# LSH attention feeding a gated MLP on one core: first late weight set fetched in the last heads, late pools with waits by tile, two orders of loads changed

## The chip, the cores and the metric

The kernel runs on one core of a Trainium2 chip. The metric is the device time of one execution in microseconds, with the median over runs. The engines are named as the profile names them: PE (TensorE matmuls), PEld (its weight loads), DVE (VectorE), ACT (ScalarE), POOL (GpSimd) and SP (SyncE, which here issues nearly all DMAs).

## The reference

Attention over 4 batches of 8 heads, 768 positions and 64 columns, masked to pairs whose hash buckets agree, and behind it a gated MLP on the 3072 tokens.

```python
q_bits = (np.einsum('bhsd,dk->bhsk', q, proj) > 0)          # 6 bits, and the same for k
mask = q_bucket[:, :, :, None] == k_bucket[:, :, None, :]
scores = np.where(mask, scale * np.matmul(q, k.transpose(0, 1, 3, 2)), -1e9)
attn = np.exp(scores - np.max(scores, axis=-1, keepdims=True))
attn = attn / (np.sum(attn, axis=-1, keepdims=True) + 1e-09)
x = np.matmul(attn, v)                                       # to (3072, 512)
gate = 1.0 / (1.0 + np.exp(-(x @ w_gate)))                   # w_gate, w_val: 512 x 1536
out = (gate * (x @ w_val)) @ w_out                           # w_out: 1536 x 512
```

q, k, v and the projection are fp32; the three MLP weights are passed as 64-bit floats.

## The kernel before, in words

**Precision.** Each fp32 operand of a large product is split in a high and a low fp32r part, and a product takes three matmuls (low times high, high times low, high times high). This is why each tile below comes as a pair: `xh` and `xl`, `a11h` and `a11l`, `gh` and `gl`. The high part is a cast on ACT, the low part a subtraction on POOL or DVE.

**Attention (first half of the program).** Sixteen pairs of heads `(b, hp)` run one after the other, each in two groups `g` of three query tiles, so 96 score steps in all. A step is `sc` (PE), `e` (DVE, the maximum and a copy), the exponent (ACT); a group then is turned (`tp`, PE), copied (`ef`, ACT or DVE) and multiplied with v (`pv`, PE). The group's row sums go to DRAM and come back broadcast (`rd`, then `rb`, both DMAs from SP), POOL multiplies `xs` with `rb`, and a DMA stores the result as `xd`, the attention output turned. Names end in batch, head pair and group: `xs3_3_1` is the last.

**Weight preparation, in the gaps of attention.** Each of 12 column blocks per matrix is loaded (`raw`, 512 KB), converted from 64-bit integers to fp32 (`ex`, `mf`; DVE, ACT, POOL in turn), split in two and, for the blocks `J1` = 2 and up, stored to DRAM (`kg`, `kv`, `ko`). Blocks of gate and value are first combined in pairs, as the 7-product scheme below wants them. Ten of 12 blocks are prepared during attention, the last two in the late half. `W_KEY` = 12 is the score step at which the first of them becomes due, and `W_STEP` = 2.2 the distance.

**Early MLP units.** Eight units `(b, g)` of 384 tokens compute the share of the first two 128-wide column blocks: `load_x` fetches `xr` (two DMAs of 384 KB) from `xd` and splits it to `xh` and `xl`; then come `zg` and `zv` (PE, L500; two blocks each, 12 matmuls per block), the gate, `gh` and `gl`, and `zo` (PE, L533; three token tiles of 6 matmuls), stored as `part`. The first six fill gaps of attention. The last two, `3_0` and `3_1`, come after the last head: `3_1` needs `xr3_1`, whose buffer is free only when POOL has made the last `xl` of `3_0`.

**Late MLP (second half).** The other ten column blocks are taken in five sets of two, three sets in phase 0 and two in phase 1; in each phase the four batches follow one another (`moe_pair`). A batch's x is loaded as four blocks `ra11`, `ra12`, `ra21`, `ra22` (384 KB each), and four sums of them (`s1` to `s4`) are made, for the 7-product (Strassen-Winograd) scheme: per set and matrix seven steps `z1` to `z7` of 6 matmuls (L719), in the order 1, 2, 5, 6, 3, 7, 4. `yo` (L838) is the product with w_out. The first set of the first batch is block pair 4: `z1g` and `z2g` need only a11 and a12 of batch 0 and the piece `wg0_4`. `fetch_piece` loads a set's ten pieces (two times three of 512 KB and one of 256 KB, and two of 512 KB: 4608 KB).

**What sets the order.** The whole program is put in order before it is built, by `Plan`: tasks with keys, modelled durations, dependencies and a stock of buffers are laid on the five engines, and each engine then executes its list strictly in that order. A wait in front of one instruction holds all that stands behind it on the same engine; SP's list of DMAs is one of these.

**The switch between the halves.** Attention's pools (`attn`, `stage1`, PSUM `ps2`) are held by the stack `ph1`. The task `switch` closes them and opens the late pools `latex`, `latet`, `latew` and `ps3` in the same memory. It runs when all `xd` stores (`every`) and all prepared weights (`early_kept`) are done, and all late fetches come after it.

```python
later["switch"] = add(0, "sp", 0, switch, after=every + early_kept, give=["moe"] * 2)
```

Of the kernel before, what the change touches and what calls it, by code (L numbers as in the profile page):

```python
# [42 lines left out]
class Task:  # L43
# [7 lines left out]
    def __init__(self, key, options, after, take, give, tail, kind):  # L51
        self.key, self.options, self.take, self.give, self.tail = key, options, take, give, tail
        self.kind, self.tiles = kind, DIVISION[kind]
        self.started, self.then, self.waits = False, [], 0
        for a in after:
            if a is not None:
                a.then.append(self)
                self.waits += 1
        self.ready = 0


class Plan:
# [9 lines left out]
    def add(self, key, engine, ns=None, emit=None, after=(), take=(), give=(), tail=0, kind="all"):  # L72
        options = engine if isinstance(engine, list) else [(engine, ns, emit)]
        t = Task((key, len(self.tasks)), options, after, take, give, tail, kind)
        self.tasks.append(t)
        return t

    def order(self):
# [24 lines left out]
        while events:  # L103
# [10 lines left out]
            while again:  # L114
                again = False
                for e in SEEN:
# [39 lines left out]
                    for r in t.give:  # L156
                        at(seen, "give", r)
                    for a in t.then:
# [11 lines left out]
def lsh_attention_glu_kernel(ctx, tc, q, k, v, proj, w_gate, w_val, w_out, out):  # L170
# [84 lines left out]
    stage1 = ph1.enter_context(tc.tile_pool(name="stage1", bufs=1))  # L255
# [18 lines left out]
    stock = dict(  # L274
        one=1, two=3, moe=1, z=6, kr=2, qr=2, vr=2, h=2, e=12, st=3, su=3, sv=2, rb=2, xs=2,
        ef=4, qx=1, kx=1, raw1=1, cv1=1, wk1=2, raw2=1, cv2=1, wk2=1, xr=1, x=1, ob=3, ol=3, sn=4, sg=6, gf=4, sc=1, port=1,
# [27 lines left out]
    def converted(key, n, j, late, which, after, first):  # L304
# [9 lines left out]
        def load():  # L314
            z["raw"] = raw = stage().tile([P, 2 * N_EL], I32, name=f"raw{n}{j}", tag="wraw")
# [223 lines left out]
    def moe_early(key, b, g, stored, pace):  # L539
# [8 lines left out]
        for j in range(J1):  # L548
# [6 lines left out]
            ))  # L555
        if direct:
# [38 lines left out]
        return prev, last_z  # L595
# [3 lines left out]
    def x_pair(u, b, last_use):  # L599
# [38 lines left out]
        def raw(name):  # L638
            got[name] = dma(
                FIRST, 393216, lambda: load(name), after=stored[b, int(name[1]) - 1] + [later["switch"]], take=[f"r{name}"],  # L640
            )
# [22 lines left out]
        pieces_of("a12")  # L664
# [14 lines left out]
    def fetch_piece(at_, js, slot, n, m, after, first):  # L679

        def go():
# [3 lines left out]
            else:  # L685
                to = later["x"].tile([P, 2, size], F32R, name=f"w{n}{m}_{js[0]}_{at_[0]}{at_[1]}", tag=f"w{slot}{n}{m}")
# [7 lines left out]
            after=[made_piece[key_], later["switch"], last_fetch.get(role)] + after, take=[role],  # L694
# [208 lines left out]
    score_tasks = {}  # L903
# [10 lines left out]
    def pair(i):  # L914
# [6 lines left out]
        def load(n, eng):  # L921

            if n == "k":
                z[n] = at.tile([P, 2, GT, 2, D], F32, name=f"kr{u}", tag="kr", bufs=stock["kr"])
# [4 lines left out]
            else:  # L929
                z[n] = at.tile([P, NC, 2, D], F32, name=f"qr{u}", tag="qr", bufs=stock["qr"])  # L930
# [22 lines left out]
        def plain_(n, eng):  # L953
            z[n + "x"] = at.tile([P, S], F32, name=f"{n}x{u}", tag=f"{n}x", bufs=1)
# [72 lines left out]
        for m, n in enumerate("qk"):  # L1027
# [5 lines left out]
            add(0, "sp", 0, lambda: None, after=[c_, a], give=[n + "x"])  # L1033
            needs.append(c_)
# [171 lines left out]

    units = [(b, g) for b in range(B) for g in range(NG)]
    PARTS = 2 * J1 + GT
    for m, (b, g) in enumerate(units):
# [6 lines left out]
        last_early, last_x = moe_early(1e4 + m, b, g, stored[b, g], [p if p is None else score_tasks[p] for p in pace])  # L1216
# [16 lines left out]
    for i, sets in enumerate(PHASES):  # L1233
        for b in range(B):
            for js, slot in sets:
                alone = sum(x[1] == slot for x in sets) == 1
                for n, m in PIECES:
                    if alone and b:
                        made[(i, b), js, n, m] = made[(i, 0), js, n, m]
                    else:  # L1240
                        fetch_piece((i, b), js, slot, n, m, [last_early] if (i, b) == (0, 0) and slot == 1 else [], (i, b) == (0, 0))
# [34 lines left out]
```

## Time and profile before

| what | value |
|---|---|
| median of 3 runs (lowest to highest) | 1017.61 us (1016.65 to 1025.71) |
| the profiled execution's own time | 1016.87 us |
| its span, first to last instruction | 1014.9 us |
| PE, DVE, ACT, POOL busy | 979.6, 762.2, 559.9, 288.2 us |
| attention's last `pv` ends, late half's last store lands | about 513 us, about 1011 us |

A profile's page gives the busy time of each engine, then the span in 40 equal slices (25.4 us each) with a digit for tenths of busy time; `PEclk` is the TensorE clock granted in a slice. A row of the timeline has a start and a duration in us, engine, line, operation, the tiles out and in, and in brackets how long the engine had been idle before and what released it. A row of the windows view has, for one stretch, its length, the busy time of each engine with the number of instructions, the granted clock, the busy share of the DMA engines and the GB/s moved. Line numbers are those of the kernel before.

### The profile page before, as it was taken

What the parts mean: (1) busy time and instruction counts of PE and PEld (TensorE: products, weight loads), DVE (VectorE), ACT (ScalarE), POOL (GpSimd) and SP (SyncE); (2) the same over time, 40 slices, a digit from 0 to 9 for tenths busy, and PEclk for the clock granted to TensorE, in tenths of its full rate; (3) what the DMA queues carried; (4) which work ended last, traced back from release to release, by engine and by line L of the source; (5) the groups of instructions that cost most, each with busy time, mean ns of one, the idle gap of its engine ahead of it and who ended that gap; (6) DMA issues with size and microseconds to landing.
All of it is one profiled execution on the core that took longest, in us unless ns stands there. A gap on an engine that the chain in (4) does not pass through costs nothing.

```text
span 1014.9 us, 20971 instructions
## 1 busy us (share of the span) xinstructions
PE 979.6 (97%) x8108; PEld 779.9 (77%) x8108; DVE 762.2 (75%) x1412; ACT 559.9 (55%) x1022; POOL 288.2 (28%) x259
## 2 busy tenths in 40 slices
PE   7999999999999999999979999999999999999998
PEld 3665566676666666675668989999989989999897
DVE  2878997898777778887615787888787778787864
ACT  1778787877677778887644352343233325242430
POOL 4024346555554366463443121211000000000000
PEclk9999999999999999999998999999999999999999
DMA  7355666576775668645467977588359671505021
GB/s 159 90 148 147 168 170 176 183 227 180 219 200 190 183 179 261 184 144 184 167 245 261 383 285 258 203 281 310 140 185 385 210 274 42 187 16 171 32 93 63
DMA packets 145988, 192.43 MB, mean 190 GB/s; under 512 B 65248, under 2 KB 104416, under 8 KB 145888
## 3 DMA queue, kind: packets, MB, share of 16 engines
q1 hardware_dynamic: 144160, 190.69, 58.3%
q8 instruction: 64, 1.05, 0.4%
q10 hardware_dynamic: 1728, 0.40, 0.2%
q14 instruction: 36, 0.29, 0.1%
HBM read 127.41 MB, written 49.28 MB: 174 GB/s over the span
## 4 chain that ended last, share of the span: by engine, by line
PE 78%; DVE 8%; DMA 6%; SPq 3%; ACT 2%; issue 1%; POOL 1%; DVEq 0%; ACTq 0%; POOLq 0%
PE yo L838 16%; PE pv L1127 11%; PE sc L1059 7%; PE tp L1110 5%; PE zo L533 3%; DVE e L1069 3%; PE sc L1053 3%; PE zg L500 3%; DMA rawv<-in_moe_w_val_dram 2%; PE zv L500 2%; PE z4g L719 2%; PE z1g L719 2%; PE z1v L719 2%; PE z4v L719 2%; PE z7v L719 2%; PE z3v L719 2%
## 5 line engine op out<-in xcount | busy, mean ns | idle before, releaser
L1077 ACT ACTIVATE e<-e,st 128x768 f32<-128x768 f32 x192 | 178.6, 932 | 47.8 <-DVE e L1069 47.0
L1069 DVE TENSOR_SCALAR_CACHE_REDUCE e<-sc 128x768 f32<-128x768 f32 x192 | 176.3, 953 | 26.9 <-PE sc L1059 26.0
L1127 PE MATMUL pv<-ef,vr 128*64 128x384 f32 x768 | 143.4, 503 | 0.8 <-DVE ef L1117 0.8
L1110 PEld LDWEIGHTS tp<-ident,e 64*128 64x128 f32 x2304 | 84.6, 139 | 36.5 <-issue 14.7
L1110 PE MATMUL tp<-ident,e 64*128 64x64 f32 x2304 | 95.3, 226 | 7.2 <-DVE e L1069 3.1
L1117 DVE COPY ef<-tp 128x768 f32<-128x768 f32 x88 | 83.0, 950 | 21.5 <-PE tp L1110 21.4
L1117 ACT COPY ef<-tp 128x768 f32<-128x768 f32 x104 | 81.3, 797 | 31.1 <-PE tp L1110 30.5
L1127 PEld LDWEIGHTS pv<-ef,vr 128*64 128x64 f32 x768 | 48.8, 138 | 57.8 <-issue 48.7
L1059 PE MATMUL sc<-kh,ql 64*128 64x384 f32 x192 | 89.8, 468 | 0.0
L1059 PE MATMUL sc<-kh,qsl 64*128 64x384 f32 x192 | 89.8, 468 | 0.0
L1053 PE MATMUL sc<-kb,qb 64*128 64x384 bf16 x384 | 66.1, 330 | 10.4 <-DMA kb<-bits 2.7
L1059 PE MATMUL sc<-kh,qh 64*128 64x384 f32 x192 | 64.3, 335 | 0.0
L1059 PE MATMUL sc<-kh,qsh 64*128 64x384 f32 x192 | 64.2, 335 | 0.0
L1059 PE MATMUL sc<-kl,qh 64*128 64x384 f32 x192 | 64.0, 333 | 0.0
L1059 PE MATMUL sc<-kl,qsh 64*128 64x384 f32 x192 | 64.0, 333 | 0.0
L1053 PEld LDWEIGHTS <-qb 64*128 64x128 bf16 x384 | 22.6, 94 | 49.7 <-issue 41.1
L1137 POOL TENSOR_TENSOR xs<-xs,rb 128x384 f32<-128x384 f32 x32 | 32.7, 1022 | 71.4 <-DVE xs L1134 60.4
L739 ACT COPY snm1g<-z1g 128x384 f32<-128x384 f32 x20 | 9.6, 481 | 76.1 <-PE z1g L719 76.1
L838 PE MATMUL yo<-wo,gh 128*128 128x512 f32 x144 | 44.6, 391 | 0.0
L877 DVE TENSOR_TENSOR ol<-yo,ol 128x512 f32<-128x512 f32 x36 | 24.7, 687 | 23.4 <-PE yo L838 22.8
L500 PE MATMUL zg<-xh,wg 128*128 128x384 f32 x128 | 38.7, 361 | 3.6 <-ACT xh L470 3.6
L1059 PEld LDWEIGHTS sc<-kh,qsl 64*128 64x128 f32 x192 | 37.3, 194 | 1.5 <-issue 1.5
(562 smaller groups left out, 2817.7 us busy)
## 6 DMA issues: line engine op xcount, KB each, us to landing
wg<-kg SPq DMA_DIRECT2D x33, 512.0 KB
wv<-kv SPq DMA_DIRECT2D x33, 512.0 KB
ra<-xd SPq DMA_DIRECT2D x32, 384.0 KB
wo<-ko SPq DMA_DIRECT2D x22, 512.0 KB
part<-ob SPq DMA_DIRECT2D x36, 256.0 KB
kg<-pkg SPq DMA_DIRECT2D x15, 512.0 KB
kv<-pkv SPq DMA_DIRECT2D x15, 512.0 KB
kr<-in_k_dram SPq DMA_DIRECT2D x64, 96.0 KB
```

The costliest lines, as they stand in the source:

```text
L500: nc.tensor.matmul(z["acc"][:, :GN], a[:, wc], x[xx][c // 2][:, c % 2, :], start=(c == 0 and i == 0), stop=(c == KC - 1 and i == 2),)
L533: nc.tensor.matmul(acc, a[:, slot, ts_], w, start=(first and i == 0), stop=(last and i == 2))
L719: nc.tensor.matmul(bank[m], a[:, wc], x[xx, block][:, c, :], start=(c == 0 and i == 0), stop=(c == 1 and i == 2),)
L838: nc.tensor.matmul(accs[t], a[:, ts_], w, start=(start and jj == 0 and q == 0), stop=(stop and jj == 1 and q == 2),)
L1053: nc.tensor.matmul(sc[:, j, :GN], z["qb"][rows, c], z["kb"][rows, h], start=True, stop=False, tile_position=(j * D, 0),)
L1059: nc.tensor.matmul(sc[:, j, :GN], q_[rows, c], z["k" + x][rows, h * GN : (h + 1) * GN], start=False, stop=(m == 2), tile_position=(j * D, 0),)
L1069: nc.vector.tensor_scalar(sp(e), gz["sc", t, h][:, :, :GN], MASKED, None, op0=ALU.min, op1=ALU.min, accum_out=gz["st", t][:, h : h + 1],)
L1077: nc.scalar.activation(e, e, AF.Exp, bias=st[:, h : h + 1], scale=-1.0, accum_out=gz["su"][:, h * GT + t : h * GT + t + 1],)
L1110: nc.tensor.transpose(tp[:, r, at_ : at_ + D], gz["e", t, h][rows, c * P : (c + 1) * P], ident[rows, rows], tile_position=(r * D, 0),)
L1117: copy(gz["ef", c].rearrange("p (n r d) -> p r n d", r=2, d=D), gz["tp", c][:, :, :GN].rearrange("p r (n d) -> p r n d", d=D),)
L1127: nc.tensor.matmul(gz["pv"][rows, :GN], z["v"][:, h, c], gz["ef", c][:, h * GN : (h + 1) * GN], start=(c == 0), stop=(c == NC - 1), tile_p ...
L1137: nc.gpsimd.tensor_mul(gz["xs"], gz["xs"], gz["rb"])
```

## The change

Six edits are made together.

1. `stage1` gets a stack of its own, `ph0`, on the right side of the memory, and the tiles of the first steps of a head (`kr`, `qr`, `qx`, `kx`) move into it from `attn`. When all early weights are kept and all heads' q and k are split and hashed (`heads_done`), a new task `first` closes `ph0` and opens the pool `latep` there. The first late set's pieces (slot 0) are fetched into `latep` after `first`, no longer after `switch`.
2. The late pools are opened with `reuse_waits="tile"`: a new tile waits for the instructions that used the memory under it, not for the whole pool.
3. `switch` no longer waits until the `xd` stores are done, only until they have started in the plan (`begun`, `at_start`).
4. The late x blocks get the key `FIRST + 0.5`, behind the early unit's `xr` (`FIRST`); they are loaded in the order a11, a12, a21, a22, and a12 is split directly behind a11.
5. Weight preparation starts at step 6 instead of 12, and `raw` has two buffers instead of one while attention runs.
6. The slot 1 pieces of the first batch wait for the earlier of the last unit's `zg` and `zv` that free their memory, not all for its end.

```diff
-    stage1 = ph1.enter_context(tc.tile_pool(name="stage1", bufs=1))
+    ph0 = ExitStack()
+    stage1 = ph0.enter_context(tc.tile_pool(name="stage1", bufs=1, side="right"))
...
-    W_KEY, W_STEP = 12.0, 2.2
+    W_KEY, W_STEP = 6.0, 2.2
...
-        ... raw1=1, cv1=1, ...
+        ... raw1=2, cv1=1, ...
...
-                FIRST, 393216, lambda: load(name), after=stored[...] + [later["switch"]], take=[f"r{name}"],
+                FIRST + 0.5, 393216, lambda: load(name), after=stored[...] + [later["switch"]], take=[f"r{name}"],
...
-        for name in ("a11", "a21", "a22", "a12"):
+        for name in ("a11", "a12", "a21", "a22"):
             raw(name)
         ready = z["ready"]
         pieces_of("a11")
+        pieces_of("a12")
...
-                to = later["x"].tile([P, 2, size], F32R, ...)
+                to = later["x" if slot else "p"].tile([P, 2, size], F32R, ...)
...
-            after=[made_piece[key_], later["switch"], last_fetch.get(role)] + after, take=[role],
+            after=[made_piece[key_], later["switch" if slot else "first"], last_fetch.get(role)] + after, take=[role],
...
+    def first_switch():
+        ph0.close()
+        later["p"] = ctx.enter_context(tc.tile_pool(name="latep", bufs=1, side="right", reuse_waits="tile"))
+
+    later["first"] = add(0, "sp", 0, first_switch, after=early_kept + heads_done)
...
-            later[n] = ctx.enter_context(tc.tile_pool(name=f"late{n}", bufs=1))
-        later["ps"] = ctx.enter_context(tc.tile_pool(name="ps3", bufs=6, space=PSUM))
-
-    later["switch"] = add(0, "sp", 0, switch, after=every + early_kept, give=["moe"] * 2)
+            later[n] = ctx.enter_context(tc.tile_pool(name=f"late{n}", bufs=1, reuse_waits="tile"))
+        later["ps"] = ctx.enter_context(tc.tile_pool(name="ps3", bufs=6, space=PSUM, reuse_waits="tile"))
+
+    later["switch"] = add(0, "sp", 0, switch, after=[later["first"]], begun=every, give=["moe"] * 2)
...
-                        fetch_piece(..., [last_early] if (i, b) == (0, 0) and slot == 1 else [], (i, b) == (0, 0))
+                        first = (i, b) == (0, 0) and slot == 1
+                        free = last_g if (n, m) in (("g", 0), ("g", 1)) else last_x if (n, m) in (("g", 2), ("v", 0)) else last_early
+                        fetch_piece(..., [free] if first else [], first)
```

What this makes of the engines' lists is seen at three places. The first is SP's list of DMAs between the stores of the last heads and the x of the last early unit. Before (`ra110` is block a11 of batch 0, `xr03_1` the first half of x of unit 3_1, `part2` a store of an early unit, `wg0_4` the first piece of the first set):

```order
L1140 DMA xd3_65<-xs3_3_1_8616 128x384
L590 DMA part2_100<-ob0_2_1_8632 128x512
...
L617 DMA ra110_0_8683<-xd0_62 128x2x384
L617 DMA ra210_0_8685<-xd0_62 128x2x384
L463 DMA xr03_1_8690<-xd3_65 128x2x384
L463 DMA xr13_1_8691<-xd3_65 128x2x384
L617 DMA ra220_0_8705<-xd0_62 128x2x384
L617 DMA ra120_0_8710<-xd0_62 128x2x384
L864 DMA ol0_0_0_8716<-part0_98 128x512
L688 DMA wg0_4_00_8722<-kg4_0_116 128x1024
```

And now:

```order
L1151 DMA xd3_65<-xs3_2_1_8306 128x384
L698 DMA wg0_4_00_8385<-kg4_0_116 128x1024
...
L1102 DMA rd31_97<-sv3_3_1_8426 4x32x32
...
L1109 DMA rb3_3_1_8497<-rd31_97 64x384 x2
L1151 DMA xd3_65<-xs3_3_0_8519 128x384
...
L1151 DMA xd3_65<-xs3_3_1_8640 128x384
...
L627 DMA ra110_0_8691<-xd0_62 128x2x384
...
L627 DMA ra120_0_8705<-xd0_62 128x2x384
...
L627 DMA ra210_0_8712<-xd0_62 128x2x384
L472 DMA xr03_1_8717<-xd3_65 128x2x384
L472 DMA xr13_1_8718<-xd3_65 128x2x384
```

The ten pieces of the first set moved from behind the x loads to behind the store of `xs3_2_1`, six of them ahead of `rd31` and four behind it. In front of `xr03_1` there are now three x blocks instead of two, each with a `part2` store ahead of it; a12 moved from behind `xr` to ahead of it.

The second place is ACT's list at the same point. Before:

```order
L629 CAST a11h0_0_8727<-ra110_0_8683 128x768
L520 CAST gh_212<-gf0_3_0_8747 128x384
L629 CAST a12h0_0_8760<-ra120_0_8710 128x768
L470 CAST xh03_1_8763<-xr03_1_8690 128x384
L629 CAST s1h0_0_8768<-sc0_0_8754 128x768
L470 CAST xh03_1_8763<-xr03_1_8690 128x384
L520 CAST gh_212<-gf1_3_0_8777 128x384
L470 CAST xh13_1_8764<-xr13_1_8691 128x384 x2
```

And now:

```order
L639 CAST a11h0_0_8734<-ra110_0_8691 128x768
L562 ACTIVATE sig_209<-zg1_3_0_8721 128x384
L639 CAST a12h0_0_8753<-ra120_0_8705 128x768
L529 CAST gh_212<-gf0_3_0_8770 128x384
L479 CAST xh03_1_8789<-xr03_1_8717 128x384 x2
L529 CAST gh_212<-gf1_3_0_8794 128x384
L479 CAST xh13_1_8790<-xr13_1_8718 128x384
L749 COPY snm1g4_0_0_8812<-z1g4_0_0_8782 128x384
```

The cast of a12 still stands ahead of those of x, and now also ahead of the first `gh` of unit 3_0; the cast of `s1` moved from between the casts of x to behind them.

The third place is PE's list behind the last product of unit 3_0 (`zv1_3_0`). Before:

```order
L500 MATMUL zv1_3_0_8736<-xh13_0_8627,wv1_2106 128x384
L533 MATMUL zo0_3_0_8772<-wo0_2314,gl_213 128x512
...
L500 MATMUL zg0_3_1_8785<-xh03_1_8763,wg0_1423 128x384
...
L533 MATMUL zo1_3_0_8808<-wo0_2314,gl_213 128x512
...
L719 MATMUL z1g4_0_0_8824<-a11h0_0_8727,wg0_4_00_8722 128x384
...
L533 MATMUL zo2_3_0_8839<-wo0_2314,gl_213 128x512
...
L500 MATMUL zg1_3_1_8852<-xh03_1_8763,wg1_1678 128x384
```

And now:

```order
L509 MATMUL zv1_3_0_8763<-xh13_0_8651,wv1_1646 128x384
L729 MATMUL z1g4_0_0_8782<-a11h0_0_8734,wg0_4_00_8385 128x384
...
L542 MATMUL zo0_3_0_8796<-wo0_1889,gl_213 128x512
...
L729 MATMUL z2g4_0_0_8803<-a12h0_0_8753,wg0_4_00_8385 128x384
...
L509 MATMUL zg0_3_1_8814<-xh03_1_8789,wg0_1042 128x384
...
L542 MATMUL zo1_3_0_8833<-wo0_1889,gl_213 128x512
...
L542 MATMUL zo2_3_0_8852<-wo0_1889,gl_213 128x512
...
L509 MATMUL zg1_3_1_8863<-xh03_1_8789,wg1_1205 128x384
```

Two late steps, `z1g` and `z2g` of the first set, moved in front of the first product of unit 3_1.

More of the change, by code (lines that the diff above doesn't have):

```diff
@@ L43, with __init__ @@
 class Task:
-    def __init__(self, key, options, after, take, give, tail, kind):
+    def __init__(self, key, options, after, take, give, tail, kind, begun):
         self.key, self.options, self.take, self.give, self.tail = key, options, take, give, tail
         self.kind, self.tiles = kind, DIVISION[kind]
-        self.started, self.then, self.waits = False, [], 0
+        self.started, self.then, self.at_start, self.waits = False, [], [], 0
         for a in after:
@@ L58, in __init__ @@
                 self.waits += 1
+        for a in begun:
+            a.at_start.append(self)
+            self.waits += 1
         self.ready = 0
@@ L70, in __init__, with add @@
         self.landings = [0] * IN_FLIGHT
-    def add(self, key, engine, ns=None, emit=None, after=(), take=(), give=(), tail=0, kind="all"):
+    def add(self, key, engine, ns=None, emit=None, after=(), take=(), give=(), tail=0, kind="all", begun=()):
         options = engine if isinstance(engine, list) else [(engine, ns, emit)]
-        t = Task((key, len(self.tasks)), options, after, take, give, tail, kind)
+        t = Task((key, len(self.tasks)), options, after, take, give, tail, kind, begun)
         self.tasks.append(t)
@@ L157, in order @@
                         at(seen, "give", r)
+                    for a in t.at_start:
+                        a.waits -= 1
+                        a.ready = max(a.ready, now)
+                        if not a.waits:
+                            at(a.ready, "ready", a)
                     for a in t.then:
@@ L314, in load @@
         def load():
-            z["raw"] = raw = stage().tile([P, 2 * N_EL], I32, name=f"raw{n}{j}", tag="wraw")
+            z["raw"] = raw = stage().tile([P, 2 * N_EL], I32, name=f"raw{n}{j}", tag="wraw", bufs=1 if late else stock["raw1"])
             if n == "o":
@@ L639, in raw @@
             got[name] = dma(
-                FIRST, 393216, lambda: load(name), after=stored[b, int(name[1]) - 1] + [later["switch"]], take=[f"r{name}"],
+                FIRST + 0.5, 393216, lambda: load(name), after=stored[b, int(name[1]) - 1] + [later["switch"]], take=[f"r{name}"],
             )
@@ L685, in go @@
             else:
-                to = later["x"].tile([P, 2, size], F32R, name=f"w{n}{m}_{js[0]}_{at_[0]}{at_[1]}", tag=f"w{slot}{n}{m}")
+                to = later["x" if slot else "p"].tile([P, 2, size], F32R, name=f"w{n}{m}_{js[0]}_{at_[0]}{at_[1]}", tag=f"w{slot}{n}{m}")
             pieces[js, n, m] = to[:, 0], to[:, 1]
@@ L1215, in lsh_attention_glu_kernel @@
             pace = [None] * PARTS
-        last_early, last_x = moe_early(1e4 + m, b, g, stored[b, g], [p if p is None else score_tasks[p] for p in pace])
+        last_early, last_x, last_g = moe_early(1e4 + m, b, g, stored[b, g], [p if p is None else score_tasks[p] for p in pace])
     def switch():
```

17 lines of the change are left out of this document (9 added, 8 removed).

## The prediction

> **What bounds the kernel now.** I read the page first: which engine is busy, and in which slices it is not.
>
> ```profile
> PE 979.6 (97%) x8108; PEld 779.9 (77%) x8108; DVE 762.2 (75%) x1412; ACT 559.9 (55%) x1022; POOL 288.2 (28%) x259
> PE   7999999999999999999979999999999999999998
> PEclk9999999999999999999998999999999999999999
> ```
>
> PE sets the time: the change removes no matmul, so all it can give back is PE's idle time (1014.9 - 979.6 = 35.3 us) and the time at a lower granted clock. Inside the program the 21st slice stands out for PE (7) and the 22nd for the clock (8): there, around 530 us, the halves meet. I then asked the windows view for that place, for the two dips of attention, and for the late half.
>
> ```profile
> 276.00:284.00 8.00, 6.11 (x46) 4.10 (x42) 4.20 (x8) 6.65 (x12) 5.60 (x4) 0.79 0.91 248
> 475.60:482.20 6.60, 4.92 (x43) 2.56 (x42) 4.96 (x10) 4.87 (x9) 1.07 (x1) 0.74 0.40 151
> 526.00:538.00 12.00, 6.09 (x14) 3.68 (x15) 5.86 (x5) 4.04 (x8) 7.20 (x6) 0.65 1.03 401
> 591.00:1009.00 418.00, 417.58 (x2185) 388.81 (x2185) 320.63 (x560) 146.73 (x275) 19.69 (x16) 1.00 0.52 182
> ```
>
> The columns are PE, PEld, DVE, ACT, POOL busy, then clock, DMA share, GB/s. After 591 us PE idles 0.42 us in 418: nothing is left there. At 526 to 538 it idles 5.9 us, and the clock of 0.65 says that much of its work ran at half speed. The two dips of attention have the same shape: 1.7 to 1.9 us idle, then some 4 us at half clock. Such a dip costs 8.00 - 6.11 + 0.21 x 8.00 = 3.6 us, or 6.60 - 4.92 + 0.26 x 6.60 = 3.4 us.
>
> The Trainium skill ("TensorE: Matmul & The Clock Gate", part 1) gives the half clock to a PE that was idle for a window of about 3.4 us; the trace disagrees, since it shows half clock after less than 2 us. By the page a dip would cost its idle time alone, 1.7 us, and the sum below would end about 1 us higher.
>
> **The switch, wait by wait.** PE's timeline with the first and last product of unit 3_0 (517.28, 525.45), to the second `zg` of unit 3_1:
>
> ```profile
> 517.28 0.33 PE L500 MATMUL zg<-xh,wg 128*128 128x384 f32 x1
> 525.45 0.34 PE L500 MATMUL zv<-xh,wv 128*128 128x384 f32 x1
> 526.90 0.50 PE L533 MATMUL zo<-wo,gl 128*128 128x512 f32 x1 [1.11 <-POOL gl L521]
> 531.47 0.69 PE L500 MATMUL zg<-xh,wg 128*128 128x384 f32 x1 [3.61 <-ACT xh L470]
> 541.01 0.33 PE L719 MATMUL z1g<-a11h,wg 128*128 128x384 f32 x1
> 542.05 0.39 PE L533 MATMUL zo<-wo,gl 128*128 128x512 f32 x1
> 543.44 0.33 PE L500 MATMUL zg<-xh,wg 128*128 128x384 f32 x1
> 545.52 0.33 PE L500 MATMUL zv<-xh,wv 128*128 128x384 f32 x1
> ```
>
> From the starts of the last four rows: a late step (6 matmuls) takes 542.05 - 541.01 = 1.04 us, a token tile of `zo` 543.44 - 542.05 = 1.39, a `zg` of 12 matmuls 2.08. Between 525.79 and 543.44, in 17.65 us, PE does three `zo` tiles, one `zg` and one step: 4.17 + 2.08 + 1.04 = 7.29 us of work. **10.4 us are lost here.** Why, is in the rows of the engines that PE waits for:
>
> ```profile
> 513.65 1.00 POOL L1137 TENSOR_TENSOR xs<-xs,rb 128x384 f32<-128x384 f32 x1
> 515.83 2.96 POOL L474 TENSOR_TENSOR xl<-xr,xh 128x384 fp32r<-128x384 f32 x3 [0.19 <-ACT xh L470]
> 525.85 0.99 POOL L521 TENSOR_TENSOR gl<-gf,gh 128x384 fp32r<-128x384 f32 x1 [7.07 <-ACT gh L520]
> 522.93 0.84 ACT L629 CAST a11h<-ra 128x768 fp32r<-128x768 f32 x1 [0.78 <-DMA ra<-xd]
> 530.18 0.83 ACT L629 CAST a12h<-ra 128x768 fp32r<-128x768 f32 x1 [4.40 <-DMA ra<-xd]
> 530.91 0.51 ACT L470 CAST xh<-xr 128x384 fp32r<-128x384 f32 x1
> ```
>
> ```profile
> 482.93 0.61 SPq L1091 DMA_DIRECT2D rd<-sv  x1
> 490.85 0.32 SPq L1140 DMA_DIRECT2D xd<-xs  x1
> 495.77 0.58 SPq L1091 DMA_DIRECT2D rd<-sv  x1
> 511.48 0.33 SPq L384 DMA_DIRECT2D ko<-pko  x1
> 514.69 0.33 SPq L1140 DMA_DIRECT2D xd<-xs  x1
> 515.36 3.05 SPq L590 DMA_DIRECT2D part<-ob  x3
> 518.59 1.99 SPq L617 DMA_DIRECT2D ra<-xd  x2
> 520.68 0.92 SPq L463 DMA_DIRECT2D xr<-xd  x2
> 521.65 0.98 SPq L617 DMA_DIRECT2D ra<-xd  x2
> 523.31 4.04 SPq L688 DMA_DIRECT2D wg<-kg  x4
> ```
>
> The chain: PE waits 3.61 us for ACT's `xh`; ACT stands at `a12h`, which is ahead of it in ACT's list, and waits 4.40 us for a12. That block is the last of four x loads (issued by 522.6, landed at 530.2), followed closely by weights at 401 GB/s.
>
> **The change part by part, term 1: the switch.** SP issues a11 and a12 earlier: they stand behind the first and second `part` store, which begin at 515.36, so at about 516 and 517 us. a11 took 522.93 - 518.59 = 4.3 us from issue to ACT, a12 in the flood 7.6; so they are there by 520.5 and by 521 to 525. The weights needed first are already in memory. `xr` of unit 3_1 is in fact not ahead of the x blocks: it waits for POOL's last `xl` of unit 3_0 (515.83 + 2.96 = 518.79), as before, so its two DMAs go at about 519 to 520. Ahead of them in flight are at most three x blocks and two stores, 1.7 MB, 4.2 us at 401 GB/s, so x is there at about 525.
>
> Then, with the durations above and 1.0 us per POOL operation, PE's new list runs so: `z1g` 525.8 to 526.8; the first half of `zo0` (its `gl` is ready at 526.84) to 527.5; `z2g` to 528.6; meanwhile POOL makes `xl` (527.9), `gl` (528.9), and three more `xl` (529.9, 530.9, 531.9). PE takes a quarter of `zg0` (0.52) to 529.1, half a `zo0` to 529.8, a quarter to 530.4, `zo1` to 531.8, the other half of `zg0` to 532.9, `zo2` to 534.2. So `zg1` starts at 534.2 instead of 543.44, with `z2g` done in addition: **9.2 + 1.0 = -10.2 us**. Nothing but PE's own work lies on this path; the closest wait has 0.1 us of slack (POOL's pace), the next 0.2. If x lands at 529.6, as late after its issue as ACT's cast came in before (530.91 - 521.1 = 9.8, an upper bound), PE idles 2.5 us and runs 4 us at half clock: -5.7. I take -10.2, since the 4.5 MB of weights that shared the DMA engines are gone; ends -5.7 and -10.4.
>
> **Term 2: the late stall.** In the late half one raw load stops DVE:
>
> ```profile
> 570.08 0.38 SPq L320 DMA_DIRECT2D rawg<-in_moe_w_gate_dram  x1
> 579.12 0.43 DVE L329 TENSOR_SCALAR exg<-rawg 128x512 int32<-128x512 int32 x1 [3.61 <-DMA rawg<-in_moe_w_gate_dram]
> 590.20 0.44 PE L719 MATMUL z4g<-a22h,wg 128*128 128x384 f32 x1 [1.31 <-DVE snuv L744]
> ```
>
> This `raw` stood in SP's list behind `wg0_6`, which waits for PE; now it stands ahead of it, directly behind the last piece of the second set. Its load is issued some 10 us earlier in PE's progress, and DVE's wait of 3.6 us goes, with it PE's 1.3 us: **-1.3**; ends 0 (if the load still comes late) and -1.7 (with the 0.42 us after 591).
>
> **Term 3: attention.** The second dip starts where DVE waits for a raw load that one buffer and SP's list made late:
>
> ```profile
> 471.22 0.39 SPq L320 DMA_DIRECT2D rawv<-in_moe_w_val_dram  x1
> 476.47 0.43 DVE L329 TENSOR_SCALAR exv<-rawv 128x512 int32<-128x512 int32 x1 [1.25 <-DMA rawv<-in_moe_w_val_dram]
> 477.82 1.47 PE L1110 MATMUL tp<-ident,e 64*128 64x64 f32 x24 [1.69 <-DVE e L1069]
> ```
>
> DVE's scores stood 1.25 us behind `exv`, and PE idled 1.69. With a second buffer the load is issued before its predecessor is used up, and preparation comes 6 of 96 steps (about 6 x 514.69 / 96 = 32 us) earlier: this dip goes, 3.4 us. But all of preparation now meets other heads' work, and the first dip, which begins with an ACT cast behind a weight store, shows what an unlucky meeting costs: 3.6 us. Bounds: -5 (both dips and some small waits gone) to +3.6 (the one gone, two new). I take **-2.0**, the dip removed less a 40% chance of a new one.
>
> **Term 4: the fetch in the last heads, at nothing.** The last prepared block `ko9` was stored at 511.48; 32 us earlier is about 480. In SP's list it now stands behind the `rd` of 482.93. So the ten pieces follow the store of 490.85 and are 4608 KB, 11.5 us at 401 GB/s: done at about 503. What covers them is PE's attention work and the DMA engines' spare time:
>
> ```profile
> 480.00:500.00 20.00, 19.87 (x219) 13.59 (x216) 14.18 (x29) 14.40 (x27) 10.09 (x11) 0.95 0.38 141
> ```
>
> At 0.38 busy there is room for them. The row sums of the last group (`rd` at 495.77) queue behind six pieces, and their `rb` behind four more; they are needed by POOL's multiplication at 513.65. Ends: 0 and one dip, +3.5, if that cover fails. Edits 2, 3 and 6 (waits by tile, `begun`, the earlier release of slot 1) let the loads of term 1 and the second set come early; the second set was not waited for by PE before, so its share is 0.
>
> **The sum**, against the profiled execution: 1016.87 - 10.2 - 1.3 - 2.0 = 1003.4. The median of the runs shown is 0.7 us above that execution: **1004.1 us**.
>
> **Rivals.** *A new wait takes half of term 1.* ACT's list holds the casts of a12, then `gh`, then x; if a12 or x lands after 526, `gh`, `gl`, `zo0` and the `sg` chain wait behind it. For it: the rows above show ACT doing just that; against it: the weights are out of the way. With the low end of term 1: 1004.1 + 4.5 = 1008.6 us.
>
> *Attention loses what the switch gains.* One or two new dips as at 276: for it, every engine's list is redrawn from step 6 on; against it, preparation is no denser. Term 3 at +3.6 and term 4 at +2: 1004.1 + 5.6 + 2 = 1011.7 us.
>
> *The early fetch holds up the end of attention (slower).* SP's list is strict: `ko9` now stands ahead of the last `rb`, `xd` and `xr` of unit 3_0. If preparation does not move up by 32 us because DVE or ACT has no room for it, SP stands at `ko9` until about 511 instead of 484. Then the `xd` of 490.85 and all ten fetches come 20 us late, `xr3_0` waits behind 11.5 us of them and lands near 528, where PE needs it at 517.28: 10.7 us idle and 2 at half clock, which more than cancels terms 1 and 2: 1017.6 - 11.5 + 12.7 = 1018.8. It decides from the point where `ko9` comes after about 495. Against it: DVE is at 14.18 of 20 us in the row above. The Trainium skill ("DMA: Bandwidth & Descriptors", "Queues, rings and completion order") says that each DMA engine consumes a queue's descriptors in order, which makes this rival worse: small transfers cannot pass the pieces. No row of the trace before shows a small transfer behind ten large ones.
>
> *The change does not do what it says.* `xr` is not ahead of the late blocks, as shown; if x and not a12 was what landed at 530, term 1 gives only the two steps moved forward, 2.1 us: 1012.2 us. Against it: ACT waited for a12 by name.
>
> **How the numbers follow.** Chances: the forecast 0.58 (its own range 1000 to 1007.4), half of term 1 lost 0.14, attention 0.13, nothing at the switch 0.08, the slower case 0.05, a larger gain 0.02. The range leaves out 2 in 10: below, -10.4 - 1.7 - 5 gives 1017.6 - 17.1 = 1000.5, to which 1.5 us are added for small waits: 999.0; above, it takes in the first two rivals: 1012.0. A change of 1% (10.2 us) is about what a measurement of this kernel can tell from none; faster by more means below 1007.4: the forecast, the larger gain and a third of the first rival, 0.64. Slower by more than 1% needs over 1027.8, more than the slower case's own price: 0.03. Between, 0.33.
>
> **What would show it.** Right: 9 for PE in the 21st slice and for the clock in the 22nd; `z1g` directly behind `zv` of 3_0, no wait over 1 us on `xh`; ten `wg`, `wv`, `wo` loads issued between 491 and 504; no wait of DVE on `rawg` near 560. Wrong: `a12h` or `xh` on ACT waiting for a DMA at 523 to 530; a late `rb` in front of POOL's last `xs`; more than one dip of the clock in attention; `ko9` after 495.

## The result and the profile after

| what | before | after |
|---|---|---|
| median (lowest to highest), 4 runs each | 1017.13 us (1014.76 to 1025.71) | 1004.31 us (1002.80 to 1007.03) |
| profiled execution, its span | 1016.87, 1014.9 us | 1004.71, 1002.8 us |
| mean granted clock of that execution | 0.991 | 1.000 |

The ratio is 0.988, with a 95% interval of 0.984 to 0.992. The kernel before has one run more here than in the prediction, so its median is 1017.13 and not 1017.61 us. The page's first rows after the change:

```profile
PE 975.5 (97%) x8108; PEld 776.2 (77%) x8108; DVE 758.5 (76%) x1407; ACT 561.1 (56%) x1027; POOL 287.2 (29%) x259
PE   7999999999999999999999999999999999999998
PEclk9999999999999999999999999999999999999999
```

The 7 in PE's 21st slice and the 8 of the clock in the 22nd are gone. To see where the 12.1 us of span came from, I cut both executions at the same two points of PE's work: the first product of unit 3_0 (517.28 before, 509.71 after) and the first `z1g` of the second late set (567.39 and 552.35). The windows view of the kernel before, then of the changed one; the columns are those of the prediction's windows.

```profile
0.00:517.28 517.28, 493.85 (x5576) 328.56 (x5577) 397.80 (x784) 383.82 (x691) 248.50 (x226) 0.99 0.61 177
517.28:567.39 50.11, 43.99 (x218) 39.65 (x216) 25.11 (x35) 20.36 (x37) 14.58 (x12) 0.90 0.83 296
567.39:1014.90 447.51, 441.80 (x2317) 411.68 (x2316) 339.31 (x594) 155.68 (x294) 25.17 (x22) 1.00 0.54 192
```

```profile
0.00:509.71 509.71, 491.18 (x5577) 326.86 (x5577) 391.51 (x779) 384.96 (x696) 250.20 (x226) 1.00 0.64 189
509.71:552.35 42.64, 40.75 (x217) 37.75 (x216) 26.47 (x36) 20.28 (x38) 13.54 (x12) 1.00 0.79 270
552.35:1002.80 450.45, 443.57 (x2317) 411.58 (x2316) 340.50 (x593) 155.86 (x294) 23.44 (x22) 1.00 0.54 188
```

PE executes the same number of matmuls in each stage (5577, 217, 2317, give or take one). So attention gave **-7.6 us**, the switch **-7.5** (50.11 to 42.64), and the late half took **2.9 us back** (447.51 to 450.45). The forecast of 1004.1 us was met, but with other parts than I had worked out: -2.0 for attention, -10.2 for the switch, -1.3 for the late half. That the sum came out is luck.

**The switch.** PE from the first row of `zv1_3_0` (the last product of unit 3_0) and its last row, to the second `zg` of unit 3_1:

```profile
516.69 0.45 PE L509 MATMUL zv<-xh,wv 128*128 128x384 f32 x1 [0.56 <-ACT sig L562]
518.71 0.34 PE L509 MATMUL zv<-xh,wv 128*128 128x384 f32 x1
518.89 0.34 PE L729 MATMUL z1g<-a11h,wg 128*128 128x384 f32 x1
521.05 0.50 PE L542 MATMUL zo<-wo,gl 128*128 128x512 f32 x1 [0.96 <-POOL gl L530]
527.63 0.44 PE L509 MATMUL zg<-xl,wg 128*128 128x384 f32 x1 [0.31 <-POOL xl L483]
529.46 0.33 PE L509 MATMUL zg<-xh,wg 128*128 128x384 f32 x1
```

`z1g` stands directly behind `zv`. From the end of `zv1_3_0` (518.71 + 0.34 = 519.05, as 525.79 in the prediction) to the second `zg` it is 529.46 - 519.05 = 10.41 us instead of 17.65, with `z2g` done in addition. The waits that are left there, 0.96 and 0.31 us, come from POOL. Their origin, first in ACT's timeline, then in DVE's and POOL's:

```profile
515.42 0.83 ACT L639 CAST a11h<-ra 128x768 fp32r<-128x768 f32 x1 [2.85 <-DMA ra<-xd]
519.41 0.51 ACT L529 CAST gh<-gf 128x384 fp32r<-128x384 f32 x1 [1.49 <-DVE gf L525]
519.88 0.93 ACT L479 CAST xh<-xr 128x384 fp32r<-128x384 f32 x2
```

```profile
517.95 0.96 DVE L643 TENSOR_TENSOR a12l<-ra,a12h 128x768 fp32r<-128x768 f32 x1 [0.71 <-ACT a12h L639]
518.83 0.55 DVE L525 TENSOR_TENSOR gf<-zv,sig 128x384 f32<-128x384 f32 x1
520.00 0.99 POOL L530 TENSOR_TENSOR gl<-gf,gh 128x384 fp32r<-128x384 f32 x1 [8.79 <-ACT gh L529]
523.19 4.39 POOL L483 TENSOR_TENSOR xl<-xr,xh 128x384 fp32r<-128x384 f32 x3
```

`xh` waits for no DMA any more: x is there before ACT comes to it. But a11 took 515.42 - 508.46 = 7.0 us from issue to ACT (its issue is in the next fence), and a12 7.5 (509.55 to 517.08). This has two effects. `gf` of the first block stands on DVE behind `a12l`: its product `zv0_3_0` ended at about 516.1, but DVE made `a11l`, waited 0.71 us for `a12h` and made `a12l` first. So `gl` was ready at 520.99, 1.9 us behind the end of `zv1_3_0`, where I had 1.05. And `sig` of the second block now stands on ACT behind `a11h`, which cost PE 0.56 us ahead of `zv1_3_0`.

**The early fetch.** SP's list, from the last prepared block to the first x block:

```profile
480.36 0.32 SPq L393 DMA_DIRECT2D ko<-pko  x1
...
482.89 0.32 SPq L1151 DMA_DIRECT2D xd<-xs  x1
483.26 2.94 SPq L698 DMA_DIRECT2D wg<-kg  x4
...
488.68 0.58 SPq L1102 DMA_DIRECT2D rd<-sv  x1
...
490.28 0.91 SPq L698 DMA_DIRECT2D wo<-ko  x2
494.28 1.11 SPq L1109 DMA_DIRECT2D rb<-rd  x2
...
508.46 0.42 SPq L627 DMA_DIRECT2D ra<-xd  x1
```

`ko9` is stored at 480.4, and the ten pieces go between 483.3 and 491.2. The prediction's sign for this, 491 to 504, lay 8 us too late: the store of `xs3_2_1`, behind which they stand, came at 482.89 and not at 490.85, since attention itself had become faster.

**The late half.** No DVE wait on `rawg` is left near 560. PE's waits behind 552.35 are two others:

```profile
PE z2v L729 <- ACT sntg L749: 1.7, 1, 1.7
PE yo L848 <- DVE gl(0, 1)2_0_0_9426 L784: 1.2, 1, 1.2
PE z6v L729 <- DVE sg(1, 0)g L754: 0.2, 1, 0.2
```

That is 3.1 us of waits against 2.0 before (`z4g` 1.3, `z3g` 0.4, `z7g` 0.3). More of the 2.9 us is in PE's busy time, which rose by 1.8 us, from 441.80 to 443.57, for the same 2317 matmuls. I looked for matmuls that take longer and found one kind, the `yo` of the set in slot 0. PE's timeline before, at the first two products with a piece of slot 0 (`10` in the tile's name is the set), then after:

```profile
866.33 0.39 PE L838 MATMUL yo<-wo,gl(0, 0)10_1_0_12108 128*128 128x512 f32 x1
866.55 0.61 PE L838 MATMUL yo<-wo,gh(0, 0)10_1_0_12107 128*128 128x512 f32 x2
867.01 0.39 PE L838 MATMUL yo<-wo,gl(1, 0)10_1_0_12166 128*128 128x512 f32 x1
```

```profile
853.38 0.39 PE L848 MATMUL yo<-wo,gl(0, 0)10_1_0_12111 128*128 128x512 f32 x1
853.61 0.63 PE L848 MATMUL yo<-wo,gh(0, 0)10_1_0_12110 128*128 128x512 f32 x2
854.08 0.39 PE L848 MATMUL yo<-wo,gl(1, 0)10_1_0_12169 128*128 128x512 f32 x1
```

A triple took 867.01 - 866.33 = 0.68 us and takes 854.08 - 853.38 = 0.70. So do the triples of slot 0 throughout (sets 4 and 10, four batches each), and those of slot 1 keep 0.68: 8 times 12 triples at 0.02 us more are 1.9 us.

### The profile page after: what moved, and what is told of

Same layout as the page of the kernel before. It is cut to its first block, busy times and chain, and to the rows that moved or that the text cites. A ratio compares the mean times of both kernels' runs of the same rounds, so it can differ in the third digit from the quotient of the medians.

```text
span 1002.8 us, 20958 instructions
## 1 busy us (share of the span) xinstructions
PE 975.5 (97%) x8108; PEld 776.2 (77%) x8108; DVE 758.5 (76%) x1407; ACT 561.1 (56%) x1027; POOL 287.2 (29%) x259
## 3 DMA queue, kind: packets, MB, share of 16 engines
q8 instruction: 64, 1.05, 0.4%
## 4 chain that ended last, share of the span: by engine, by line
PE 76%; DVE 8%; DMA 6%; issue 3%; POOL 3%; SPq 2%; ACT 1%; POOLq 0%; DVEq 0%; ACTq 0%
PE yo L848 16%; PE pv L1138 10%; PE sc L1070 7%; PE tp L1121 5%; DVE e L1080 3%; PE sc L1064 3%; PE zv L509 2%; PE zo L542 2%; PE zg L509 2%; PE z6v L729 2%; PE z7v L729 2%; PE z4v L729 2%; PE z3v L729 2%; PE z1v L729 2%; PE z7g L729 2%
## 5 line engine op out<-in xcount | busy, mean ns | idle before, releaser
L1070 PEld LDWEIGHTS sc<-kh,ql 64*128 64x128 f32 x192 | 37.3, 194 | 2.5 <-issue 2.5
L360 POOL TENSOR_TENSOR exo<-mfo,exo 128x512 f32<-128x512 f32 x12 | 15.4, 1282 | 79.3 <-DVE exo L355 62.2
```

What stands on the lines that cost most here:

```text
L1070: nc.tensor.matmul(sc[:, j, :GN], q_[rows, c], z["k" + x][rows, h * GN : (h + 1) * GN], start=False, stop=(m == 2), tile_position=(j * D, 0),)
```

## The experiments

They ran in three groups of four, each group on one chip beside the kernel before (1018.3, 1018.05 and 1017.23 us there), so ratios are compared. "The stages" are the three stretches of the result's windows, read from one profiled execution of each kernel: end of attention, switch, late half. Edit 6, and the new place of `stage1` and the head tiles by itself, were not undone in any run, so their shares are not known.

### Edit 5 alone, and its two halves

All three start from the kernel before. b_prep has both edits below, b_key6 the first alone, b_raw2 the others.

```diff
-    W_KEY, W_STEP = 12.0, 2.2
+    W_KEY, W_STEP = 6.0, 2.2
-    ... raw1=1, cv1=1, ...
+    ... raw1=2, cv1=1, ...
-    ... name=f"raw{n}{j}", tag="wraw")
+    ... name=f"raw{n}{j}", tag="wraw", bufs=1 if late else stock["raw1"])
```

> The kernel before with edit 5 alone (preparation from step 6, two raw buffers). Theory 1, two separate gains: the preparation alone gives attention its 7.6 us (both dips of the clock gone, the last xd store at about 507 instead of 514.7), and the switch keeps its 10.4 us of idle time and half clock; so 1017.1 - 7.6 = 1009.5 us, between 1008 and 1011.5. Rival, the gain in attention hangs on the released pool or on where the tiles lie: at least one dip stays and the time is 1013 to 1017 us.

> The kernel before with preparation from step 6, still one raw buffer. Theory P, the earlier start is what edit 5 gains: as edit 5 alone, about 1010 us. Theory R, the second raw buffer is: the loads still come late to DVE, a dip of the clock stays in the last third of attention, at least 1014 us.

> The kernel before with two raw buffers, preparation still from step 12. Theory R, the second buffer is what edit 5 gains: the dip at 476 us is gone, which cost 3.4 us, 1014.5 us or less (as low as 1010 if it is all of it). Theory P, the earlier start is: 1016 to 1018 us, no gain.

| kernel before with | median | ratio to before, 95% |
|---|---|---|
| both halves (b_prep) | 1009.94 us | 0.992 (0.989 to 0.995) |
| the early start alone (b_key6) | 1021.48 us | 1.003 (1.001 to 1.005) |
| two raw buffers alone (b_raw2) | 1010.31 us | 0.992 (0.989 to 0.995) |

The second buffer is all of the gain; the early start with one buffer is a loss. The stages of b_raw2:

```profile
0.00:510.49 510.49, 490.15 (x5577) 327.39 (x5578) 392.78 (x778) 384.26 (x697) 247.69 (x225) 1.00 0.61 179
510.49:557.76 47.27, 43.08 (x217) 39.55 (x216) 25.09 (x36) 20.60 (x39) 15.09 (x13) 0.93 0.90 322
557.76:1005.30 447.54, 441.96 (x2317) 411.75 (x2316) 338.87 (x593) 155.60 (x294) 24.89 (x22) 1.00 0.54 191
```

Attention ends 6.8 us earlier, the late half is the old one to 0.03 us, and the switch still loses its clock. b_key6 has three dips in attention. What stood ahead of PE's longest wait on ACT, the wait, and its window:

```profile
161.74 0.62 ACT L374 CAST pkg<-t34g 128x512 fp32r<-128x512 f32 x1 [7.07 <-DMA kg<-pkg]
167.69 0.59 PE L1110 MATMUL tp<-ident,e 64*128 64x64 f32 x12 [4.38 <-ACT ef L1117]
```

```profile
164.00:172.00 8.00, 4.32 (x30) 1.64 (x32) 3.74 (x6) 8.00 (x18) 3.01 (x3) 0.79 0.21 80
```

PE did 4.32 us of work in these 8, at a clock of 0.79. No late load is behind this one: ACT had stood 7.07 us at a cast of the preparation, whose buffer a weight store still held, and the exponents and the copy `ef` of attention came late behind it. Two smaller dips follow at 340 and 404, and there DVE had waited for raw loads:

```profile
340.08 0.43 DVE L329 TENSOR_SCALAR exg<-rawg 128x512 int32<-128x512 int32 x1 [5.18 <-DMA rawg<-in_moe_w_gate_dram]
403.53 0.43 DVE L329 TENSOR_SCALAR exo<-rawo 128x512 int32<-128x512 int32 x1 [2.48 <-DMA rawo<-in_moe_w_out_dram]
```

Behind these PE waited 2.99 and 2.28 us for DVE.

For b_prep theory 1 gave 1009.5, right on the time, though its claim that both dips go did not hold: the first is still in its profile. The window is the same stretch of the same list of attention in b_prep and, below it, in the changed kernel:

```profile
276.00:284.00 8.00, 6.51 (x64) 4.31 (x62) 5.39 (x9) 5.57 (x7) 1.80 (x3) 0.79 0.91 256
```

```profile
276.00:284.00 8.00, 6.68 (x72) 4.49 (x73) 4.52 (x9) 5.84 (x8) 2.87 (x2) 1.00 0.91 245
```

PE idles 1.5 us in the one and 1.3 in the other; one lost the clock and the other did not. So this dip is a matter of the execution as well as of the list, and the end of attention moves with it: for this list it lies between 508.66 and 511.99 in seven executions, and at 514.78 and 515.36 in two that had two and three dips in attention. The middle of the nine is 511.66. So some 2 us of attention's 7.6 in the result are the luck of that execution (509.71), if the 517.28 of the kernel before is typical; a_noprep below, with the old preparation, has 518.26.

### The early fetch undone, in three ways

a_fetch is the changed kernel with this edit; a_noprep is the changed kernel without edit 5 (`W_KEY` 12, `raw1` 1), a_key12 the changed kernel with `W_KEY` 12 alone.

```diff
-            after=[made_piece[key_], later["switch" if slot else "first"], last_fetch.get(role)] + after, ...
+            after=[made_piece[key_], later["switch"], last_fetch.get(role)] + after, ...
```

> The changed kernel with the early fetch undone (slot 0 fetched after the switch, into the same pool); the order of the x loads is the new one and all ten pieces stand behind them. Theory B, the weights out of the way are the gain: z1g of the first set waits for its weights behind zv of 3_0 by 2 to 5 us and the following steps for theirs, 1006.5 to 1009.5 us. Theory A, a12's place is all: within 1 us of the changed kernel, 1003.3 to 1005.3 us.

> The changed kernel with edit 5 undone (preparation from step 12, one raw buffer). Theory 1 in its plain form, the gains add: only attention's 7.6 us come back, 1004.3 + 7.6 = 1011.9 us. Theory 2, the gains are tied: the last prepared block is stored at about 511 again, so the first set's weights cannot be fetched in the last heads and stand among the x loads; x of unit 3_1 is late again and 4 to 6 us of the switch's gain go too, 1016 to 1018 us, no gain left over the kernel before.

> The changed kernel with two raw buffers but preparation from step 12. The early start alone made the kernel before slower (1021.5 against 1018.1 us), the second buffer alone gave all of edit 5's gain. Theory S, the early start matters only because it ends preparation in time for the early fetch: attention stays as good (last xd store at about 508 to 511), the fetch falls among the x loads as with the early fetch undone, and the time is that kernel's, 1009 to 1012 us. Rival, the early start is of no use here either: within 1.5 us of the changed kernel, at most 1005.8 us.

| changed kernel with | median | ratio to before, 95% | stages |
|---|---|---|---|
| fetch behind the switch (a_fetch) | 1010.76 us | 0.992 (0.989 to 0.995) | 511.99, 45.99, 451.42 |
| no edit 5 (a_noprep) | 1014.67 us | 0.997 (0.994 to 0.999) | 518.26, 42.95, 450.09 |
| late start, two raw buffers (a_key12) | 1015.03 us | 0.998 (0.995 to 1.001) | 511.62, 51.65, 450.53 |

**a_fetch** is theory B, 1.3 us above its range: PE's only long wait at the switch is

```profile
524.63 0.45 PE L729 MATMUL z1g<-a11h,wg 128*128 128x384 f32 x1 [4.14 <-DMA wg<-kg]
```

and x of unit 3_1 is in time, although ten pieces stand directly behind it. By the medians, the changed kernel without the early fetch is no faster than edit 5 alone (0.992 both); of its 2.8 us shorter switch (45.99 against b_prep's 48.82), 1.8 went back in the late half (451.42 against 449.63), where its `wo` has the changed kernel's place (see below). **a_noprep** contradicts theory 2: its switch takes 42.95 us, no longer than the changed kernel's 42.64, although nine of the ten pieces are fetched behind the x loads. In its list the first piece, `wg0_4`, goes ahead of a11. So it is not ten pieces out of the way that the switch needs, but, as the comparison with a_fetch says, one piece in time, with `z1g` and `z2g` in front of `zg0_3_1` to fill the time in which x is split. By the profiled stages the gains add (518.26 is about the old end of attention, +8.6 us); the median lies 1.5 us above that execution, between the times of the two theories.

**a_key12** has `wg0_4` ahead of a11 too, and attention is good, as theory S said; but it came out 3 us above its range, with the longest switch of all. Its DVE, ACT and PE:

```profile
537.54 0.43 DVE L338 TENSOR_SCALAR exg<-rawg 128x512 int32<-128x512 int32 x1 [9.01 <-DMA part<-ob]
538.00 0.72 ACT L341 ACTIVATE exg<-exg,ebias 128x512 int32<-128x512 int32 x1 [6.50 <-DVE exg L338]
538.62 0.56 ACT L587 COPY ob<-zo 128x512 f32<-128x512 f32 x1
539.24 0.69 PE L509 MATMUL zv<-xh,wv 128*128 128x384 f32 x1 [5.05 <-ACT ob L587]
```

The first late raw load was issued at 528.26 behind nine pieces of weights. DVE stands at `exg` for it (the view names a store, but `exg` reads `rawg`), ACT stands at the next step of the same conversion, and behind that in ACT's list is the copy which frees PE's bank. PE waits 5.05 us for work that has nothing to do with it. In the changed kernel the pieces are gone by then, the raw load goes at 516.10, and `exg` at 526.63 waits for nothing. But the late load alone is not enough for the chain: in a_noprep it goes at 535.40, also behind nine pieces, and DVE's list has `exg` only at 550.16, where it waits for nothing. So a_key12's extra loss comes from the order of its own list; a late start need not bring it.

### Edits 4, 3 and 2 undone

a_order puts the key, the order of the loads and the place of a12's split back; a_begun and a_tile have one of the other two edits each, a_tile at all three places.

```diff
-                FIRST + 0.5, 393216, lambda: load(name), ...
+                FIRST, 393216, lambda: load(name), ...
-        for name in ("a11", "a12", "a21", "a22"):
+        for name in ("a11", "a21", "a22", "a12"):
```

```diff
-    later["switch"] = add(0, "sp", 0, switch, after=[later["first"]], begun=every, give=["moe"] * 2)
+    later["switch"] = add(0, "sp", 0, switch, after=[later["first"]] + every, give=["moe"] * 2)
```

```diff
-    ... tc.tile_pool(name="latep", bufs=1, side="right", reuse_waits="tile"))
+    ... tc.tile_pool(name="latep", bufs=1, side="right"))
```

> The changed kernel with edit 4 undone (x blocks with the key of xr, loaded a11, a21, a22, a12, and a12 split late). ACT's list has the cast of a12 in front of those of x again, and a12 is the last of the four blocks, but the weights are in memory. Theory A, a12's place in the loads is what held x up: ACT waits 2 to 4 us at a12h and PE as long at xh, 1006 to 1008.5 us. Theory B, only the weights in flight made a12 late: within 1 us of the changed kernel, 1003.3 to 1005.3 us.

> The changed kernel with edit 3 undone: the switch is put behind the end of the xd stores in the plan. The x loads a11 and a12 then stand behind all three part stores and a12 behind x of unit 3_1, and PE's list has zg0_3_1 whole behind zo2_3_0. If the place of the x blocks hardly matters once the weights are gone, as with edit 4 undone, the time is 1003 to 1006 us; if the switch's gain rests on loading them early, x and a12 come 3 to 4 us later, PE waits as long at z1g or z2g and the time is 1007 to 1010 us.

> The changed kernel with the waits of the late pools for the whole pool under them; the order of every engine is the changed kernel's. Theory H, the waits by tile are what lets a11, a12 and z1g start before attention's last readers are through: a11 goes 2 to 4 us later and PE waits for it at z1g, 1006 to 1008 us. Theory N, attention's readers are done by then anyway: the first late load goes at most 1 us later and nothing waits for it, within 1 us, 1003.3 to 1005.3 us.

| changed kernel without | median | ratio to before, 95% | stages |
|---|---|---|---|
| edit 4 (a_order) | 1002.91 us | 0.985 (0.982 to 0.989) | 509.10, 43.45, 448.15 |
| edit 3 (a_begun) | 1006.62 us | 0.989 (0.985 to 0.992) | 508.66, 42.11, 453.93 |
| edit 2 (a_tile) | 1007.26 us | 0.991 (0.989 to 0.994) | 511.27, 42.85, 450.78 |

All three intervals overlap that of the changed kernel. a_order contradicts theory A (it is 0.4 us below theory B's range), and with it my own reading: a12 is again the last block and again ahead of x in ACT's list, and ACT does not wait for either.

```profile
517.37 0.83 ACT L639 CAST a12h<-ra 128x768 fp32r<-128x768 f32 x1
518.11 0.51 ACT L529 CAST gh<-gf 128x384 fp32r<-128x384 f32 x1
518.52 0.92 ACT L479 CAST xh<-xr 128x384 fp32r<-128x384 f32 x2
```

Its switch takes 0.8 us longer than the changed kernel's; its late half is 2.3 us shorter, since PE waits 1.2 us there and not 3.1. So edit 4 is not shown to gain anything.

In a_begun a12 is behind x, PE waits 1.4 us for it at `z2g`, and the switch still takes 42.11 us, so it is the first of its two cases, 0.6 us above the range given; what it loses is in the late half, where its redrawn list waits 2.4, 1.5 and 1.4 us between 618 and 698. In a_tile, whose lists are those of the changed kernel word for word, a11 is issued 2.9 us behind the last `xd` store instead of 1.4, and the switch takes 0.2 us longer: theory N by the stages. That its median lies 2 us above theory N's range is not explained by the switch; the profiled execution lost 1.6 us in attention, and whether that is chance is not settled.

### The place of slot 0's weights

An unused tile of 48 (a_pad192, and a_ord_pad, which also undoes edit 4) or 24 (a_pad96) words at the end of the memory shifts `latep`:

```diff
+    pad = ctx.enter_context(tc.tile_pool(name="pad", bufs=1, side="right"))
+    pad.tile([P, 48], F32, name="pad")
```

> The changed kernel with 192 bytes per partition left unused at the end of the memory, so that the pool of the first set (slot 0) begins at the same place within 2048 bytes as the other weight pools, 1824 instead of 2016. Theory address, the place of wo in memory is why a triple of yo with a slot 0 piece takes 0.70 us where all others take 0.68: all triples at 0.68, 8 x 12 x 0.02 = 1.9 us less, about 1002.4 us. Theory pool, it is the pool, its age or what else runs beside it: the triples stay at 0.70 and the time at 1004.3 us.

> The changed kernel with 96 instead of 192 bytes left unused: slot 0's wo begins at 1920 within 2048 bytes, 0 within 128, where the other pools stand at 32 within 128 and the changed kernel's at 96. If only a start 96 bytes behind a multiple of 128 is slow, the slot 0 triples of yo take 0.68 us or less; if any start other than 32 is slow, 0.70; if the slow thing is a short piece before a multiple of 2048 (32 bytes in the changed kernel, 224 with 192 bytes left unused, now 128), something between.

> The changed kernel without edit 4 and with those 192 bytes left unused: if edit 4 costs 1.4 us, as its undoing suggests, and the place of the pool 1.9 us, 1001 us; if the 1.4 us are chance, 1002.4 us; if neither is anything, 1004.3 us.

The starts are those of the memory map of each program, in bytes of a partition.

| kernel | start of `wo` in slot 0, within 2048 and within 128 bytes | triple of `yo` there | median, ratio to before |
|---|---|---|---|
| before | 800 and 1824, 32 | 0.68 us | |
| changed | 2016, 96 | 0.70 us | 1004.31 us, 0.988 (0.984 to 0.992) |
| a_pad192 | 1824, 32 | 0.68 us | 1003.58 us, 0.986 (0.983 to 0.989) |
| a_pad96 | 1920, 0 | 0.70 us | one run, 1013.31 us |
| a_ord_pad | 1824, 32 | 0.68 us | 1002.82 us, 0.985 (0.981 to 0.989) |

a_pad192 at the same products as above, and its late half:

```profile
853.20 0.39 PE L850 MATMUL yo<-wo,gl(0, 0)10_1_0_12115 128*128 128x512 f32 x1
853.42 0.62 PE L850 MATMUL yo<-wo,gh(0, 0)10_1_0_12114 128*128 128x512 f32 x2
853.88 0.39 PE L850 MATMUL yo<-wo,gl(1, 0)10_1_0_12173 128*128 128x512 f32 x1
```

```profile
552.56:1001.80 449.24, 441.84 (x2317) 411.71 (x2316) 340.51 (x593) 155.64 (x294) 23.12 (x22) 1.00 0.54 188
```

The triple is back at 0.68 and PE's busy time at 441.84 us, the old value: theory address, since the edit only moves the pools on the right side of the memory. The medians are too close to show 1.9 us by themselves. a_pad96 says that a start at 96 is not the only slow one; its time tells nothing of this, since its profile has dips of the clock at 24, 96, 284 and 636 us. a_ord_pad has the shortest late half of all (445.47 us), but its profiled attention ended at 514.78 with dips at 96 and 284. It is the version with the lowest median; that it beats the changed kernel is not shown.

## Why the prediction was right in the sum and wrong in the parts

**Term 1, predicted -10.2, measured -8.3 in the same measure** (17.65 to 10.41, and 1.04 for `z2g`). That the stretch would hold nothing but PE's own work was nearly right: 8.33 us of work (`z1g`, `z2g`, three `zo` tiles, one `zg`), 1.27 of waits, 0.8 in the seams between the interleaved pieces. The step that failed is "its `gl` is ready at 526.84", which kept the old distance between `zv` and `gl`: I followed ACT's new list and not DVE's, where `a12l` now stands ahead of `gf`. And a11 did not take 4.3 us but 7.0, a12 7.5. The whole stage gave 7.5 us, since PE also waited 0.56 us for `sig` ahead of the stretch.

The cause that I named is only half right. x was late with the old order of loads and the weights in flight together: PE waited 3.6 us at `xh` in the kernel before and 2.1 in b_prep. It was in time with the old order and the weights gone (a_order), and also with the new order and ten or nine pieces behind it (a_fetch, a_noprep). So either of the two is enough, and the place of a12, to which the prediction gave as much room, is worth nothing once the weights are gone. (a_fetch and a_noprep keep edits 2 to 4 together; which of these brings x in time there is not shown.) With x in time, what decides is whether `wg0_4` is there when `zv` of 3_0 ends: PE waits 4.14 us for it in a_fetch, not at all in a_noprep.

**Term 2, predicted -1.3, measured +2.9.** The stall named went as forecast. What failed is the silent assumption that the rest of the late half stays as it is: 1.9 us went into the place of `wo` in memory, and PE's waits rose by 1.1. The diff said `side="right"`; I read it as a question of room, not of speed.

**Term 3, predicted -2.0, measured -7.6.** The second dip went for the reason given, the second buffer. The failed step is "the dip removed less a 40% chance of a new one": it left the first dip standing and most small waits too. Of the 7.6 us, 4.9 are idle time of PE (517.28 - 493.85 = 23.4 before, 509.71 - 491.18 = 18.5 after) and 2.7 its busy time, as its clock no longer falls. That the first dip was missing is in part luck, since b_prep has it with the same list. b_raw2 gives 6.8 us without any earlier start, so it is the buffer that takes most of this out; that the early start would bring preparation into unlucky meetings is right for one buffer (b_key6, +3.4 us) and not for two.

**Term 4, predicted 0, measured 0.** `ko9` came at 480.4 where I had about 480. The cover held although the small transfers did suffer: from the last group's `rd` to its `rb` SP took 495.77 to 497.83 before, 2.1 us, and with six pieces ahead of `rd` 488.68 to 494.28, 5.6 us (a_fetch, without the pieces: 2.0). The Trainium skill ("DMA: Bandwidth & Descriptors", "Queues, rings and completion order") says that each DMA engine consumes a queue's descriptors in ring order. The trace agrees with it here, though transfers that merely share the DMA engines' time could look the same. The delay did not matter, because POOL came to the last group's multiplication only at 506.08, directly behind other work, and its store was not late.

**The rivals.** None took place as priced. The slower one failed at its own condition (`ko9` after 495). Term 1 lost a fifth, not half, and by the way that the first rival named only in part: a12 landed before `zv` ended, and the chain to `gl` was late all the same. Attention gained.

**The clock.** The Trainium skill ("TensorE: Matmul & The Clock Gate", part 1) calls its activity window free-running. If what an idle stretch does depends on where in that window it falls, the two rows at 276 to 284 above, nearly the same idle time with and without the loss, are what one would see; no run here shows the window itself. Its rule of about 3.4 us of idle time does not describe them, since the one that lost the clock idled 1.5 us in 8.

## What to carry to other kernels

Cut both executions at the same instructions and compare stage by stage before believing that a forecast was right: here three errors of about 2, 4 and 6 us cancelled by luck. When a stall is removed, follow the released order on every engine that touches it, DVE as well as ACT, and ask of each moved buffer where it now lies, not only whether it fits. A second buffer in front of a conversion with strict engine orders can be worth more than moving that conversion earlier, and without it moving earlier can lose.

## What the runs showed of the hardware

The time of a fp32r matmul with 512 moving columns depends on where its moving operand starts: 0.68 us for three at a start of 32 within 128 bytes, 0.70 us at 96 and at 0. Only three places within 128 bytes occurred, so which property of the address decides is open. The steps `z1` to `z7`, which have x as the moving operand and the weights as the stationary one, kept their pace in slot 0 too: the seven gate steps of set 4 in the third batch took 714.26 - 706.98 = 7.28 us before and 700.88 - 693.61 = 7.27 after.

Half clock followed 1.5 us of idle time in 8 in one execution and not 1.3 in another of the same list. Runs with such dips tend to be the longer ones: of the four runs of the changed kernel, three at a mean clock of 1.000 took 1002.8 to 1004.7 us, the one at 0.998 took 1007.0. In a_tile the two at 1.000 took 1004.3 and 1006.6, the one at 0.995 took 1012.7. It is no rule: the shortest run of a_begun, 1002.2 us, was at 0.998.
